# When the maxima of batch 0's v, their factor and two conversion factors come later in the program

## The chip, the cores and the metric

The kernel runs on one core of a Trainium2 chip. The metric is the time of one execution on the device in microseconds (us). The engines go by short names: PE is TensorE (matmuls and transposes), DVE is VectorE, ACT is ScalarE, POOL is GpSimd, and SP is the queue that issues the DMA transfers.

## The reference

Causal attention over 4 batches of 12 heads (448 tokens, 64 values a head), then a feed-forward layer with a leaky ReLU, then a soft mixture of eight experts:

```python
scores = scale * np.matmul(q, k.transpose(0, 1, 3, 2))
scores = np.where(mask, -1000000000.0, scores)
attn = softmax(scores)                      # over the keys
x = heads side by side of np.matmul(attn, v)   # 1792 x 768
h = x @ w_in                                # 768 x 2048
g = np.maximum(0.01 * h, h)
x = g @ w_out                               # 2048 x 768
...
logits = x @ phi                            # 768 x 32, then 8 experts of 4 slots each
return c @ slot_out                         # 1792 x 768
```

## The kernel before

The work is cut into four stages. In stage 0 (the first 100 us) the attention of batch 0 runs alone; in stages 1 to 3 the attention of batch b runs between the feed-forward matmuls of batch b-1; then come the last batch and the experts. The change touches stage 0 alone.

**Attention.** Two heads make a pair; batch 0 has pairs 0 to 5. Step n of the attention has three slots, which end at a `yield`. In step n the engines make the weights of pair n, the row maxima of pair n+1 and the product of pair n-1 with v. For pair n, in order: `qkps` (PE transposes q and k; ACT copies them, DVE subtracts for a low part, both into `qkt`); `S_3`, `S_0`, `S_1` (PE scores for the maxima, tiles 3, then 0 and 2, then 1) and `junk` on DVE, which leaves the maxima in `mxe`; `mps` (PE transposes `mxe`); `mr` (ACT, four instructions); `T_0`, `T_1`, `T_2` (PE, the scores less their maxima); `P` (ACT, the exponential; one for each T); a mask on `P` by POOL (L449) after T_1 and after T_2; `tsum` on POOL (L454, then L458 twice); `O` (PE, the product with v; its second half reads the P of T_2); `dn` (PE, the sums), `r` (DVE, reciprocal), `rb` (PE) and `rs` (ACT); at the end DVE multiplies `O` by `rs` and by batch 0's factor `s_v` (L520), and ACT and POOL split the result into the two halves of `x16`. S and T share two PSUM buffers, O has one.

**Factor of v.** `reduce_v(n)` takes the largest |v| of pair n (DVE, L370). `v_scale(b)` takes the largest over six pairs (L375), multiplies it with the identity on PE to bring it to all partitions (`v_ps`, L140), and makes the factor with five small DVE instructions. Batch 0's six maxima and its factor stand ahead of step 0 in the program.

**Conversions.** Six blocks of w_in, i0 to i5, are turned from doubles into two halves of 16 bits each in stage 0. `prep_in` is a generator; prep_step lets it go on once before (BEFORE) and once behind (AFTER) each slot. One conversion is: ACT takes the magnitude (`cv`) and the sign (`cs`) of the raw block; DVE takes its maximum (`w_am`, L228), shifts (L229) and joins the low word (L230); two AFTERs later PE multiplies the maximum with the identity (`w_ps`) and DVE makes the factor `w_s`; then ACT scales `cs` by it, POOL multiplies `cv` by `cs` (L249), ACT or POOL casts the high half of `w`, and POOL subtracts for the low half (L258). There are two buffers for `cs`, four for `cv`, three for the raw blocks.

**What sets the order.** On PE every matmul that goes through `mm` keeps the order of the program (`in_order`). On DVE, ACT, POOL and SP the order in stage 0 is that of a scheduler which plays the program through once with its own costs, except where `tc.issue_after` ties an instruction behind another. Attention slots have a higher priority (AHEAD) than conversions. At run time each engine takes its instructions strictly in the order so fixed.

Of the kernel before, what the change touches and what calls it, by code (L numbers as in the profile page):

```python
# [29 lines left out]
def as_float(bits):  # L30
    return struct.unpack("<f", struct.pack("<I", bits))[0]
# [3 lines left out]
def tile_attn_moe_softmoe(ctx: ExitStack, tc: tile.TileContext, q, k, v, w_in, w_out, phi, w1, w2, out, dbg=None):  # L35
    nc = tc.nc
# [10 lines left out]
    NP = H // 2  # L47
# [10 lines left out]
    ident = const.tile([128, 128], F32, name="ident")  # L58
# [29 lines left out]
    def ps_tr(name, shape=(128, 512)):  # L88
        return psum.tile(list(shape), F32, tag="tr", bufs=TR[0], name=name)
# [4 lines left out]
    def last_on(engine):  # L94
        return next(i for i in reversed(nc.cur_bb.bb.instructions[-400:]) if i.engine == engine)
# [35 lines left out]
    mm = partial(in_order, nc.tensor.matmul)  # L131
# [3 lines left out]
    def pow2_scale(absmax, name, shift=23, bias=0, out=None):  # L135


        ps = ps_tr(f"{name}_ps", (128, 128))
        op = nc.tensor.matmul if name == "v0" else mm
        op(ps, absmax.to_broadcast([128, 128]), ident, start=True, stop=True)  # L140
        m1 = const.tile([128, 1], F32, tag="p2_m1", bufs=2, name=f"{name}_m1")
        nc.vector.tensor_reduce(m1, ps, AX.X, ALU.max)
        nc.vector.tensor_scalar(m1, m1, as_float((27 + bias) << shift), None, ALU.max)
        e = const.tile([128, 1], I32, tag="p2_e", bufs=2, name=f"{name}_e")
        nc.vector.tensor_scalar(e, m1.bitcast(I32), shift, None, ALU.logical_shift_right)
        si = const.tile([128, 2], I32, tag="p2_s" + name[0], bufs=4, name=f"{name}_s")
        nc.vector.tensor_scalar(si[:, 0:1], e, -(2**23), (268 + bias) * 2**23, ALU.mult, ALU.add)
        if out is None:
            out = si[:, 1:2].bitcast(F32)
        nc.vector.tensor_scalar(out.bitcast(I32), e, 2**23, -(14 + bias) * 2**23, ALU.mult, ALU.add)  # L150
        return si.bitcast(F32)[:, 0:1], out
# [85 lines left out]
    def prep_in(u):  # L237

        f = u[1]
        am = const.tile([128, 1], F32, tag="w_am", bufs=2, name=f"w_am{f}")  # L240
        t, sg = to_f32(u, am)
        yield AFTER
        yield AFTER
        s_w, _ = pow2_scale(am, f"w{f}", 20, out=inv_w[:, f : f + 1])
        yield BEFORE
        if u[3]:
            yield BEFORE
        scalar.activation(sg, sg, AF.Copy, scale=s_w)
        nc.gpsimd.tensor_tensor(t, t, sg, ALU.mult)  # L249
        if u[3]:  # L250
            yield BEFORE
        w = t.rearrange("p (c f) -> p c f", c=NP)
        hi, lo = (w16[f // 4][:, x, :, 128 * (f % 4) : 128 * (f % 4 + 1)] for x in range(2))
        if f < EARLY[0] and f % 4 < HIP:
            nc.gpsimd.tensor_copy(hi, w)
        else:
            scalar.copy(hi, w)
        nc.gpsimd.tensor_tensor(lo, w, hi, ALU.subtract)  # L258
        ready.add(u[:2])
# [44 lines left out]
    BEFORE, AFTER = "before", "after"  # L304
# [58 lines left out]
    def reduce_v(n):  # L363

        b, hp = divmod(n, NP)
        if hp == 0:
            v_am[b] = am = const.tile([128, NP + 1], F32, tag="v_am", bufs=2, name=f"v_am{b}")
            nc.vector.memset(am, 0.0)
        with tc.issue_after(last_on(mybir.EngineType.DVE)) if b else ExitStack():
            nc.vector.tensor_reduce(v_am[b][:CP, hp : hp + 1], v_t[n], AX.XY, ALU.max, apply_absolute_value=True)  # L370

    def v_scale(b):

        am = v_am[b]
        nc.vector.tensor_reduce(am[:, NP:], am[:, :NP], AX.X, ALU.max)  # L375
        s_v[b], inv_v[b] = pow2_scale(am[:, NP:], f"v{b}")
# [177 lines left out]
    def attention_slots():  # L554


        for n in range(2):
            qk_stacks(n)
            load_qk(n + 2)
            if n == 0:  # L560
                for tiles in TILES:
                    maxima(0, tiles)
        for x in range(NP):
            reduce_v(x)
        v_scale(0)
        for n in range(NP + 1):
            here, more = n < NPAIR, n + 1 < NPAIR
            if n > 0:
                attend(n - 1)
            if here:  # L570
                lowering(n)
            if more:
                maxima(n + 1, TILES[0])
            if here:
                weights(n, 0)
            yield
            if n > 0:
                inverses(n - 1)
            if more:
                maxima(n + 1, TILES[1])  # L580
            if here:
                weights(n, 1)
            yield
            if n > 0:
                columns(n - 1)
            if here:
                weights(n, 2)
            if more:
                maxima(n + 1, TILES[2])
            if n + 2 < NPAIR:  # L590
                qk_stacks(n + 2)
                if n + 4 < NPAIR:
                    load_qk(n + 4)
            if n + NP < NPAIR:
                load_v(n + NP)
            if NP <= n + NP - 1 < NPAIR:
                reduce_v(n + NP - 1)
            yield

        for n in range(NP + 1, NPAIR + 1):  # L600
            here, more = n < NPAIR, n + 1 < NPAIR
            if more:
                maxima(n + 1, TILES[2])
            attend(n - 1)
            inverses(n - 1)
            if here:
                lowering(n)
            yield
            if here:
                weights(n, 0)  # L610
            if more:
                maxima(n + 1, TILES[0])
            if n % NP == 1 and n + NP - 2 < NPAIR:
                v_scale(n // NP)
            yield
            if here:
                weights(n, 1)
                weights(n, 2)
            if more:
                maxima(n + 1, TILES[1])  # L620
            if n + 2 < NPAIR:
                qk_stacks(n + 2)
                if n + 4 < NPAIR:
                    load_qk(n + 4)
            if n + NP < NPAIR:
                load_v(n + NP)
            columns(n - 1)
            if n + NP - 1 < NPAIR:
                reduce_v(n + NP - 1)
            yield  # L630

    TILES = ((3,), (0, 2), (1,))
    slots_of_attention = attention_slots()


# [213 lines left out]
    if True:  # L849
# [123 lines left out]
        for c in range(4):  # L973
            wo = loaded.pop(("wo", c))
            for h in range(2):
                for t in range(4):
                    nc.tensor.matmul(
                        psi[h][32 * t : 32 * t + 32], gdt[:, c, t], wo[:, t, 384 * h : 384 * (h + 1)],
                        start=c == 0, stop=c == 3, skip_group_check=True,
# [18 lines left out]
        for e in range(E):  # L998
            ph = ps2(f"ph{e}", (128, 256), tag="h", bufs=4)
            for hf in range(2):  # L1000
                wt = loaded.pop(("w1", (e, hf)))
                for t in range(3):
                    rows = wt[:, t].rearrange("k (p t) -> k p t", t=8)
                    for g in range(4):
# [3 lines left out]
                            start=hf == 0 and t == 0, stop=hf == 1 and t == 2, skip_group_check=True,  # L1008
# [87 lines left out]
        for x, (t0, nt, c0, cols) in enumerate(pieces):  # L1096
# [11 lines left out]
            for h in heads:  # L1108
                for t in range(nt):
# [3 lines left out]
                        start=t0 + t < 4, stop=t0 + t >= 8 * E - 4, skip_group_check=True,  # L1113
# [65 lines left out]
```

## Time and profile before

| | us |
|---|---|
| three runs | 646.23, 647.52, 650.63; median 647.52 |
| the profiled execution | 647.08 |
| its span in the trace | 645.40 |
| PE busy in the span | 579.7 (90%) |
| PE busy in 0 to 20, 20 to 40, 40 to 60 us | 7.72, 14.13, 17.78 of 20 each |
| POOL busy in 40 to 60 and 60 to 80 us | 15.99, 16.09 of 20 each |

The span runs from the first to the last instruction in the trace; the execution's own time holds 1.68 us more around it. PE's busy share is high over the whole, so what a change in the first 100 us is worth has to be read there: which engine each engine waits for in that stretch, and at what time the same instruction of each step starts.

### The profile page before, as it was taken

How to read it: one execution, taken by the hardware profiler on the slowest of the kernel's cores; microseconds unless marked ns; L12 is line 12 of the kernel's file. 1: busy time of each engine (PE TensorE's matmuls, PEld its weight loads, DVE VectorE, ACT ScalarE, POOL GpSimd, SP SyncE). 2: the span in 40 equal slices, each digit the busy share in tenths (PEclk: the TensorE clock that was granted, in tenths of full speed). 3: DMA queues.
4: the chain of work that ended last, by engine and by line, in shares of the span. 5: the costliest groups of instructions: out<-in, count | busy, mean ns of one | idle time of the engine just before them, and what ended most of it. 6: DMA issues, size and time to landing. Idle time of an engine off the chain costs nothing.

```text
span 645.4 us, 12376 instructions
## 1 busy us (share of the span) xinstructions
PE 579.7 (90%) x4874; PEld 333.8 (52%) x4874; DVE 367.5 (57%) x884; ACT 290.2 (45%) x570; POOL 235.3 (36%) x247
## 2 busy tenths in 40 slices
PE   3688888997999999999999999999999998999564
PEld 2455555654545566556656655554344445454233
DVE  5868757989965666656358667424657423001023
ACT  2566655678765657656446546432022112011012
POOL 5177973488585465435434334430000000000000
PEclk9989999998999999999999999999999998899998
DMA  9942237764552366653434312216969539999998
GB/s 183 283 112 66 59 77 200 217 164 132 144 162 72 107 180 217 190 158 100 113 106 104 110 56 68 75 39 231 356 244 412 194 132 422 407 423 423 408 328 316
DMA packets 108849, 125.67 MB, mean 195 GB/s; under 512 B 69368, under 2 KB 99064, under 8 KB 105208
## 3 DMA queue, kind: packets, MB, share of 16 engines
q1 hardware_dynamic: 108792, 124.90, 59.9%
q8 instruction: 38, 0.62, 0.4%
q14 instruction: 19, 0.16, 0.1%
HBM read 105.74 MB, written 19.14 MB: 193 GB/s over the span
## 4 chain that ended last, share of the span: by engine, by line
PE 64%; DMA 10%; POOL 8%; DVE 6%; ACT 6%; issue 3%; SPq 2%; ACTq 0%; POOLq 0%; DVEq 0%
PE H L102 30%; DMA w<-in_moe_w_dram 7%; PE O L102 5%; PE T L102 5%; PE g_acc L102 3%; PE dn L102 3%; PE L L102 2%; PE S L102 2%; PE qkps L102 2%; PE ph L1005 2%; DMA raw_i_None<-in_moe_w_in_dram 2%; PE wt_ps L102 2%; POOL w L258 2%; ACT P L113 2%; DVE cv_i_None L230 1%
## 5 line engine op out<-in xcount | busy, mean ns | idle before, releaser
L102 PE MATMUL H<-x,w 128*128 128x448 f16 x1152 | 229.8, 353 | 0.7 <-ACT g L113 0.7
L102 PEld LDWEIGHTS <-w 128*128 128x128 f16 x1152 | 111.0, 99 | 110.9 <-issue 17.8
L409 DVE CUSTOM_DVE_ANT_0 junk<-S,mask 112x224 bf16<-112x224 f32 (+3 forms) x192 | 85.2, 444 | 58.9 <-PE S L102 55.9
L487 DVE RECIPROCAL rs<-rs 128x224 f32<-128x224 f32 x36 | 53.4, 1524 | 40.6 <-ACT rs L113 40.6
L113 ACT ACTIVATE P<-T 112x672 f32<-112x672 f32 (+1 forms) x72 | 57.0, 793 | 22.0 <-PE T L102 20.9
L449 POOL TENSOR_SCALAR_AFFINE_SELECT P<-P 112x448 f32<-112x448 f32 x48 | 30.8, 643 | 91.2 <-ACT P L113 71.0
L102 PE MATMUL T<-qkt 64*112 64x336 f32 (+3 forms) x576 | 60.1, 321 | 4.4 <-ACT P L113 3.6
L113 ACT ACTIVATE g<-H,iv 128x448 f32<-128x448 f32 x48 | 30.5, 635 | 67.6 <-PE H L102 48.3
L102 PE MATMUL O<-P,v 112*64 112x448 f32 (+3 forms) x384 | 52.0, 410 | 4.5 <-POOL P L449 4.4
L102 PEld LDWEIGHTS T<-qkt 64*112 64x112 f32 x576 | 42.8, 180 | 14.6 <-issue 6.0
L458 POOL TENSOR_TENSOR tsum<-tsum,P 112x448 f32<-112x448 f32 (+1 forms) x48 | 47.4, 987 | 1.9
L102 PEld LDWEIGHTS O<-P,v 112*64 112x64 f32 x384 | 25.2, 138 | 29.2 <-issue 11.9
L454 POOL TENSOR_TENSOR tsum<-P 112x672 f32<-112x672 f32 x24 | 39.1, 1630 | 1.8
L102 PE MATMUL S<-qkt 64*112 64x224 f32 (+3 forms) x192 | 31.6, 369 | 7.6 <-DVE mxe L409 2.9
L997 POOL MEMSET hz<- 128x256 f32 x2 | 0.6, 312 | 97.7 <-PE g_acc L102 97.7
L113 ACT ACTIVATE g_spare<-H,iv 128x448 f32<-128x448 f32 x16 | 10.2, 635 | 56.7 <-PE H L102 56.7
L387 DVE TENSOR_TENSOR qkt<-qkps,qkt 128x448 fp32r<-128x448 f32 x48 | 29.1, 621 | 9.7 <-ACT qkt L113 9.7
L102 PE MATMUL T<-mr,onesr 64*112 64x448 f32 (+1 forms) x192 | 30.7, 316 | 4.3 <-ACT mr L113 4.3
L249 POOL TENSOR_TENSOR cv_i_None<-cv_i_None,cs_i_None 128x768 f32<-128x768 f32 x16 | 28.6, 1786 | 11.1 <-ACT cs_i_None L113 11.1
L113 ACT ACTIVATE mr<-mps,own 128x112 fp32r<-128x112 f32 x96 | 26.2, 361 | 14.0 <-PE mps L102 14.0
L113 ACT COPY rs<-dn 128x448 f32<-128x448 f32 x18 | 9.6, 533 | 50.5 <-PE dn L102 47.5
L267 POOL TENSOR_TENSOR cv_o_None<-cv_o_None,cs_o_None 128x768 f32<-128x768 f32 x10 | 16.5, 1647 | 42.4 <-DVE cv_o_None L230 18.4
(176 smaller groups left out, 906.8 us busy)
## 6 DMA issues: line engine op xcount, KB each, us to landing
w<-in_moe_w_dram SPq DMA_DIRECT2D x31, 1536.0 KB
raw_i_None<-in_moe_w_in_dram SPq DMA_DIRECT2D x16, 768.0 KB
raw_o_None<-in_moe_w_out_dram SPq DMA_DIRECT2D x10, 768.0 KB
g_far<-g SPq DMA_DIRECT2D x32, 224.0 KB
gb<-g_far SPq DMA_DIRECT2D x8, 896.0 KB
wo<-wsc SPq DMA_DIRECT2D x4, 1536.0 KB
qk<-in_q_dram SPq DMA_DIRECT2D x48, 112.0 KB
qk<-in_k_dram SPq DMA_DIRECT2D x48, 112.0 KB
```

The source lines that it names most:

```text
L102: op(*args, **kwargs)
L113: op(*args, **kwargs)
L249: nc.gpsimd.tensor_tensor(t, t, sg, ALU.mult)
L258: nc.gpsimd.tensor_tensor(lo, w, hi, ALU.subtract)
L267: nc.gpsimd.tensor_tensor(wo, wo, sg, ALU.mult)
L387: nc.vector.tensor_tensor(st[:, j, 1], p, st[:, j, 0].bitcast(F32), ALU.subtract)
L409: nc.vector.tensor_tensor_reduce(out=junk[:, :w], in0=ps[:, a, at : at + w], in1=mask[:, S - w :], scale=-1.0, scalar=3e38, op0=ALU.add, o ...
L449: nc.gpsimd.affine_select(out=d, in_=d, compare_op=ALU.is_ge, fill=0.0, base=0, pattern=[[0, 4], [1, CP]], channel_multiplier=-1,)
L454: nc.gpsimd.tensor_tensor(tsum[:CP], p[0][:CP, :, 0, CP:], p[0][:CP, :, 1, : S - CP], ALU.add)
L458: nc.gpsimd.tensor_tensor(y, y, p[1][:CP, :, j, : S - CP * (j + 2)], ALU.add)
L487: nc.vector.reciprocal(rs[:, c : c + S // 2], rs[:, c : c + S // 2])
L1005: nc.tensor.matmul(ph[32 * g : 32 * g + 32].rearrange("s (p u) -> s p u", u=2), sit[:, 3 * hf + t], rows[:, :, 2 * g : 2 * g + 2], start=h ...
```

## The change

The six reductions of batch 0's v leave the place ahead of step 0. Two of them come into the second slot of step 0, four into the third, and the factor into the third slot of step 1. Each reduction is tied behind the DVE instruction that the program issued last before it. The product `v_ps` goes through `mm`, so it now has its fixed place among PE's instructions. For i0 and i1 the product `w_ps` comes two slots later than before.

```diff
         ps = ps_tr(f"{name}_ps", (128, 128))
-        op = nc.tensor.matmul if name == "v0" else mm
-        op(ps, absmax.to_broadcast([128, 128]), ident, start=True, stop=True)
+        mm(ps, absmax.to_broadcast([128, 128]), ident, start=True, stop=True)
...
         yield AFTER
         yield AFTER
+        if f < 2:
+            yield AFTER
+            yield AFTER
         s_w, _ = pow2_scale(am, f"w{f}", 20, out=inv_w[:, f : f + 1])
...
+        behind = last_on(mybir.EngineType.DVE)
         if hp == 0:
...
-        with tc.issue_after(last_on(mybir.EngineType.DVE)) if b else ExitStack():
+        with tc.issue_after(behind):
             nc.vector.tensor_reduce(v_am[b][:CP, hp : hp + 1], v_t[n], AX.XY, ALU.max, apply_absolute_value=True)
...
-        for x in range(NP):
-            reduce_v(x)
-        v_scale(0)
         for n in range(NP + 1):
...
+            if n == 0:
+                reduce_v(0)
+                reduce_v(1)
             yield
+            if n == 1:
+                v_scale(0)
             if n > 0:
                 columns(n - 1)
...
+            if n == 0:
+                for x in range(2, NP):
+                    reduce_v(x)
```

The scheduler's order changes with it on every engine in stage 0. PE, ahead of step 0, before (`v0_ps` is the product of v's maximum, `mps0` the transpose of pair 0's maxima; the digit after a name is the pair or conversion):

```order
L102 MATMUL qkps1_1_241<-ident_64,qk1_162 128x112 x4
L140 MATMUL v0_ps_262<-ident_64,v_am0_253 128x128
L102 MATMUL mps0_272<-ident_64,mxe0_142 128x112
L102 MATMUL S1_3_279<-qkt1_233 112x448 x2
L102 MATMUL T0_0_286<-qkt0_186 112x448 x6
```

PE, in step 1, of the changed kernel:

```order
L102 MATMUL T1_1_447<-qkt1_233 112x336 x6
L102 MATMUL T1_1_447<-mr1_391,onesr_120 112x336 x2
L139 MATMUL v0_ps_464<-ident_64,v_am0_312 128x128
L102 MATMUL rb0_474<-r0_432,first_131 64x112 x8
L102 MATMUL T1_2_489<-qkt1_233 112x224 x6
```

The product with v's maximum has left the place ahead of `mps0` and stands behind T_1 of pair 1, in front of `rb0`.

ACT, from the first `mr` on, before:

```order
L113 ACTIVATE mr0_274<-mps0_272,own_123 128x112 x4
L113 ACTIVATE cv_i0_None_297<-raw_i0_None_179 128x768
L113 ACTIVATE cs_i0_None_298<-raw_i0_None_179 128x768
L113 ACTIVATE cv_i1_None_396<-raw_i1_None_181 128x768
L113 ACTIVATE cs_i1_None_397<-raw_i1_None_181 128x768
L113 ACTIVATE P0_448_144<-T0_0_286 112x2x448
L113 ACTIVATE cv_i2_None_557<-raw_i2_None_183 128x768
L113 ACTIVATE P0_448_144<-T0_1_319 112x2x336
```

and in the changed kernel:

```order
L113 ACTIVATE mr0_255<-mps0_253,own_123 128x112 x4
L113 ACTIVATE P0_448_144<-T0_0_267 112x2x448
L113 ACTIVATE P0_448_144<-T0_1_300 112x2x336
L113 ACTIVATE cv_i0_None_278<-raw_i0_None_179 128x768
L113 ACTIVATE cs_i0_None_279<-raw_i0_None_179 128x768
L113 ACTIVATE P0_224_145<-T0_2_316 112x2x336
L113 ACTIVATE cv_i1_None_371<-raw_i1_None_181 128x768
L113 ACTIVATE cs_i1_None_372<-raw_i1_None_181 128x768
```

The first two exponentials of pair 0 no longer stand behind two conversions.

ACT, in step 2, of the changed kernel (in the kernel before, only `cv_i5` stands between these two exponentials):

```order
L113 ACTIVATE P0_448_144<-T2_0_585 112x2x448
L113 ACTIVATE cs_i1_None_372<-cs_i1_None_372,w1_s_559 128x768
L113 ACTIVATE cs_i2_None_544<-cs_i2_None_544,w2_s_606 128x768
L113 ACTIVATE cv_i4_None_871<-raw_i4_None_378 128x768
L113 CAST w16_0_97<-cv_i1_None_371 128x6x128
L113 ACTIVATE cs_i3_None_716<-raw_i3_None_285 128x768
L113 CAST w16_0_97<-cv_i2_None_543 128x6x128
L113 ACTIVATE cs_i4_None_872<-raw_i4_None_378 128x768
L113 ACTIVATE P0_448_144<-T2_1_633 112x2x336
```

POOL, at the same place, in the changed kernel:

```order
L461 TENSOR_TENSOR tsum_148<-tsum_148,P1_224_147 112x2x112
L251 TENSOR_TENSOR cv_i1_None_371<-cv_i1_None_371,cs_i1_None_372 128x768
L251 TENSOR_TENSOR cv_i2_None_543<-cv_i2_None_543,cs_i2_None_544 128x768
L260 TENSOR_TENSOR w16_0_97<-cv_i1_None_371,w16_0_97 128x6x128
L260 TENSOR_TENSOR w16_0_97<-cv_i2_None_543,w16_0_97 128x6x128
L452 AFFINE_SELECT P0_448_144<-P0_448_144 112x4x112
L457 TENSOR_TENSOR tsum_148<-P0_448_144 112x672
L525 TENSOR_TENSOR x16_0_485<-rs1_658,x16_0_485 128x448
L452 AFFINE_SELECT P0_224_145<-P0_224_145 112x4x112
```

The four POOL instructions of i1 and i2 stand together between step 1 and step 2; before, i1's stand in step 1 and i2's in step 2, and i0's in step 0 instead of step 1. From step 4 on the orders of PE, ACT and POOL are those of before (but for one transpose of PE near the end of the program), and DVE's differ in a few single instructions.

## Rows read from the trace of the kernel before

**Rows 1.** The chain that ended last, 20 to 66 us, summed by line.

```profile
by line: DMA raw_i_None<-in_moe_w_in_dram 29.1%; issue 18.1%; POOL tsum L458 11.3%; POOL cv_i_None L249 10.6%; POOL tsum L454 10.6%; POOL w L258 10.6%; POOL P L449 8.3%; POOL x L522 4.4%; ACT cv_i_None L113 3.9%; ACT P L113 2.0%; ACT cs_i_N
```

**Rows 2.** PE's timeline: start, length (us), instruction, count, idle before and its releaser.

```profile
17.63 0.77 PE L140 MATMUL v_ps<-ident,v_am 128*128 128x128 f32 x2 [6.38 <-DVE v_am L375]
18.19 0.39 PE L102 MATMUL mps<-ident,mxe 112*128 112x112 f32 x1
...
25.00 1.18 PE L102 MATMUL T<-qkt 64*112 64x336 f32 x6 [3.56 <-ACT P L113]
...
40.52 1.76 PE L102 MATMUL rb<-r,first 128*64 128x112 f32 x16
...
44.06 0.36 PE L102 MATMUL S<-qkt 64*112 64x224 f32 x2 [0.66 <-DVE mxe L409]
...
47.30 0.32 PE L102 MATMUL mps<-ident,mxe 112*128 112x112 f32 x1
...
52.41 0.99 PE L102 MATMUL rb<-r,first 128*64 128x112 f32 x16 [0.59 <-DVE r L497]
...
58.22 0.32 PE L102 MATMUL mps<-ident,mxe 112*128 112x112 f32 x1
...
61.84 0.41 PE L102 MATMUL dn<-tsum,sixteen 128*64 128x112 f32 x4 [0.52 <-POOL tsum L458]
```

**Rows 3.** ACT's timeline, conversions and the first exponential.

```profile
20.21 0.91 ACT L113 ACTIVATE cv_i_None<-raw_i_None 128x768 f32<-128x768 f32 x1 [0.43 <-DMA raw_i_None<-in_moe_w_in_dram]
...
24.05 0.89 ACT L113 ACTIVATE P<-T 112x896 f32<-112x896 f32 x1
...
42.76 0.94 ACT L113 ACTIVATE cs_i_None<-cs_i_None,w_s 128x768 bf16<-128x768 bf16 x1
```

**Rows 4.** DVE's timeline, the last maximum of pair 0.

```profile
13.39 0.08 DVE L409 DVE_READ_ACCUMULATOR2_ANT mxe<- 112x1 f32 x1
```

**Rows 5.** DVE by line, 0 to 110 us: count, then busy us, mean ns, idle before.

```profile
L409 DVE CUSTOM_DVE_ANT_0 junk<-S,mask 112x224 bf16<-112x224 f32 (+3 forms) x66 | 29.2, 442 | 10.3 <-PE S L102 9.2
L387 DVE TENSOR_TENSOR qkt<-qkps,qkt 128x448 fp32r<-128x448 f32 x18 | 10.6, 621 | 9.7 <-ACT qkt L113 9.7
L370 DVE TENSOR_REDUCE v_am<-v 112x1 f32<-112x512 f32 x13 | 8.9, 681 | 2.5 <-DMA v<-in_v_dram 2.5
L228 DVE TENSOR_REDUCE w_am<-cv_i_None 128x1 f32<-128x768 f32 x7 | 6.6, 938 | 0.6 <-ACT cv_i_None L113 0.6
L230 DVE SCALAR_TENSOR_TENSOR cv_i_None<-raw_i_None,cv_i_None 128x768 int32<-128x768 int32 x6 | 5.6, 935 | 0.0
...
L497 DVE RECIPROCAL r<-dn 128x112 f32<-128x112 f32 x6 | 5.1, 852 | 0.7 <-PE dn L102 0.7
L229 DVE TENSOR_SCALAR cv_i_None<-cv_i_None 128x768 int32<-128x768 int32 x6 | 4.3, 718 | 0.1
L520 DVE SCALAR_TENSOR_TENSOR rs<-O,v_s,rs 128x448 f32<-128x448 f32 x6 | 4.1, 682 | 1.0 <-ACT rs L113 1.0
```

**Rows 6.** Timeline of POOL and DVE, side by side.

```profile
27.96 1.61 POOL L454 TENSOR_TENSOR tsum<-P 112x672 f32<-112x672 f32 x1
...
28.41 1.58 DVE L229 TENSOR_SCALAR cv_i_None<-cv_i_None 128x768 int32<-128x768 int32 x1
```

**Rows 7.** POOL's timeline.

```profile
33.57 1.65 POOL L249 TENSOR_TENSOR cv_i_None<-cv_i_None,cs_i_None 128x768 f32<-128x768 f32 x1
...
45.92 1.05 POOL L522 TENSOR_TENSOR x<-rs,x 128x448 f16<-128x448 f32 x1
...
48.03 1.66 POOL L258 TENSOR_TENSOR w<-cv_i_None,w 128x768 f16<-128x768 f32 x1
...
56.85 0.59 POOL L449 TENSOR_SCALAR_AFFINE_SELECT P<-P 112x448 f32<-112x448 f32 x1
```

**Rows 8.** Stretches of 2 us: length, then busy (count) of PE, PEld, DVE, ACT, POOL; granted clock.

```profile
36.00:38.00 2.00, 0.82 (x6) 0.48 (x6) 0.00 (x0) 1.45 (x6) 1.92 (x2) 1.00 0.28 52
...
40.00:42.00 2.00, 2.00 (x22) 1.55 (x18) 1.97 (x11) 0.73 (x1) 0.56 (x1) 0.50 0.07 25
```

## The prediction

> **What bounds the kernel now.** I read the chain of work first, over 20 to 66 us. The reader is to see that no PE line is among its large shares: the five POOL lines of attention and conversions hold 11.3 + 10.6 + 10.6 + 10.6 + 8.3 + 4.4, some 56% of the stretch, and the landing of the first raw blocks 29% [rows 1]. So stage 0 is a pipeline that POOL paces once the blocks have landed. Then PE's timeline, for the waits at its start: 6.38 us until the six maxima of v are in, and 3.56 us in front of T_1 of pair 0, for the first exponential [rows 2]. That exponential starts at 24.05, because two conversions stand before it on ACT, and the first of them waits for its block until 20.21 [rows 3]. The marks by which I measure progress are the same instructions of each step: S_1 at 44.06, mps of pair 2 at 47.30, mps of pair 3 at 58.22 [rows 2]. From step 4 on PE, ACT and POOL have their old order, so a shift that stands there is carried to the end one for one; the later stages have no timetable of their own.
>
> **Removed: the wait for v, and the conversions before the first exponential.** The last maximum of pair 0 is read out at 13.39 to 13.47, and two of v's reductions (0.68 each) lie ahead of it on DVE [rows 4, 5]. Without them mps of pair 0 can run at about 13.0 (an estimate: part of their time is a wait for ACT's copies in any case) instead of 18.19 [rows 2], which is 5.2 us. Its exponentials follow at once, so the 3.56 us go too: some 8.5 us in all, if nothing else were late. Nothing of it is worth more than what comes next on the other engines, so I follow DVE and then POOL.
>
> **DVE takes the work back.** The magnitude of i0 still cannot be there before 20.21 + 0.91 = 21.1 [rows 3], and behind it DVE now has an unbroken run. Until the factor w_s of i0: three conversions' DVE part, each 0.94 + 0.55 + 0.94 (the shift's mean of 0.72 holds one long case; the other five have (4.3 - 1.58)/5 = 0.54) make 7.3; four reductions of v 2.7; six `junk`, 0.44 each and 0.08 for the read-out, 3.1; two `qkt` 1.2; the reciprocal 0.85; the small ones about 1.0, an estimate from their number, seven of 0.15 [rows 4 to 6]. That is 16.2, so w_s of i0 is there at 37.3. Two more `junk` and some small ones end at 38.5, and S_1 of pair 2 follows on PE: 38.5 against 44.06, still 5.5 us ahead. The factor of v costs nothing here beyond its DVE time, which is in the sum: PE waits for `rb` and S_1 at that place in any case, and `v_ps` is ready before T_1 is done. Behind `v_ps` on PE stand `rb`, T_2 and S_1; all wait for DVE's run, not for it. Then `rs` 0.68, two `junk` 1.0, two `qkt` 1.2, a reduction of v 0.68, i3's part 2.4, two `junk` 1.3 and small ones 0.8 bring w_s of i1 to 46.5.
>
> **POOL, and the two conversions that meet in step 2.** i0's factor moves later, so POOL can begin its product only at 37.3 + 0.94 for the scaling of the signs = 38.2, against 33.57 before [rows 3, 7]. POOL loses there 4.6 of the microseconds that PE has won. Before pair 2's first mask it must do both products and both low halves of i1 and i2, and this begins with w_s of i1: 46.5 + 0.94 + 4 x 1.65 + mask 0.59 + tsum 1.61 + x 1.05 + mask 0.59 = 57.9 [rows 3, 6, 7]. ACT takes the same path: between two exponentials of step 2 it has seven instructions instead of one, and one of them casts what POOL has just made, so the exponential of T_1 ends near 53.5. Before, that last mask ended at 56.85 + 0.59 = 57.44 and mps of pair 3 came 0.78 later [rows 2, 7]; now 57.9 + 0.8 = 58.7 against 58.22. So all 5.5 us are given back within step 2, and 0.5 more.
>
> **What DVE and POOL do to each other.** One shift on DVE took 1.58 instead of 0.54 us: it began while POOL's tsum ran and ended 0.42 after it, at 29.99 against 29.57 [rows 6]. In the new order, POOL's tsum of pair 1 runs at about 35 to 36.7, beside i2's joining on DVE, and i0's low half at about 43.3 to 45, beside i3's shift. No row shows a joining (L230) begin beside a running POOL instruction. By the one row each place costs 0 to 1.0 us, so 0 to 2.0 together; I take 1.0, since the shift is the form that was seen to wait and the joining is not. The Trainium skill, page "SBUF — State Buffer", section "Who interferes with whom", says that DVE and GpSimd share one pair of ports as an exclusive lock, and that a DVE instruction with two inputs in SBUF meets it too. By that rule both places would wait and the sum would be about 1 us higher than mine.
>
> **The sum.** mps of pair 3: 0.5 later from the chain above, and 1.0 for the wait between DVE and POOL: +1.5. In the trace of before the sums `dn` then waited 0.52 us for POOL's last tsum [rows 2], which now comes behind no low half; that wait goes: some -0.6. Net +0.9 on the profiled execution's 647.08, so **648.0 us**. The runs shown have a median of 647.52 and reach from 646.23 to 650.63, so the profiled execution is one of the middle. About 1% (6.5 us) is what a measurement of this kernel can tell from no change, and I forecast no change. The parts not priced: the transpose that changes places near the end, and single DVE reductions of later batches, stand in work with slack on both sides; they get 0, with a few tenths either way if that cover is gone. On the SP queue the fourth raw block now goes behind the loads of pair 4's q and k, some 2 us later than before by the places of its neighbours (an estimate). Its magnitude stands on ACT between the first and the second exponential of pair 1, and T_1 of that pair, which waits for DVE's run until 32 to 33.5, hides it; if that cover is gone it costs those 2 us at S_1 of pair 2, where 5.5 are in hand.
>
> **Rivals.** (1) The lead is kept. If the two conversions of step 2 fill time in which PE waits for nothing, the lead at mps of pair 2 stands to the end. S_1 at 38.5, then 0.4 for itself, 1.7 for qkps (slow like the `rb` of that time), 0.5 for w_ps of i1 and 2.1 for O give 43.3 against 47.30 [rows 2], 4.0 us: 647.1 - 4.0 = 643.1. For it: POOL was idle at several places in each step, as the 18% "issue" in the chain shows [rows 1]. Against it: the exponential of T_1 stands behind all of them on ACT, in strict order. (2) Slower, by PE's clock. In step 2 PE waits some 2.9 us in front of `rb` and 2.3 in front of T_2. In the trace of before, a stretch with PE busy for only 0.82 of 2 us (36 to 38) was followed by one at a granted clock of 0.50 (40 to 42), the level of 1.2 GHz [rows 8]; `rb` took 1.76 there and 0.99 in the next step [rows 2]. T_2, S_1, qkps and O of one step, 4.1 us at the full clock, would take some 6.4 (an estimate: up to 1.8 times as long, as `rb`, and less where weight loads set the pace). This decides once T_2 starts later than about 53: then PE and no longer POOL is last, and mps of pair 3 comes at 55.4 + 6.4 = 61.8, net +3.0: 650.1. The Trainium skill, "TensorE: Matmul & The Clock Gate", section "What's actually happening", says the low level is the default and activity lifts it; by that rule this rival holds if the two waits count as idle. (3) All is kept: 647.1 - 8.5 = 638.6, if DVE's run is far shorter than my sum. Against it: the sum is made of measured lengths. (4) The change does not do what it says, and the wait for v only moves to `v_ps` in step 1: PE would then stand there until L375, which I place at 29; `v_ps` comes at 33.5. The price is nil, and the time as in the forecast.
>
> **How the numbers follow.** Forecast, within -1.5 and +1.5 of 648.0: 0.46, with 0.03 of it for (4). Rival 1: 0.22. Rival 2: 0.25. Rival 3: 0.04. The rest, 0.03, is for what the later stages might make of a shift. The range takes in rivals 1 and 2 at their centres with half a microsecond for the runs' spread: 642.8 to 650.6. Only rival 3 and a part of the rest are over 1% faster: 0.05; over 1% slower is a part of rival 2 and of the rest: 0.03; 0.92 lie within 1%.
>
> **What would show it.** In the profile of the changed kernel: mps of pair 0 at 13 (first step right); S_1 of pair 2 near 38.5 with DVE without a gap from 21 to 38 (second); POOL's first product near 38 and four conversion instructions in a row between 46 and 55 (third); the exponential of T_1 of pair 2 ending near 53.5 and mps of pair 3 between 58 and 62. If mps of pair 3 is at 54 to 55, rival 1 is right; if PE's granted clock falls to 0.50 around 52 to 58, rival 2. The forecast is wrong if DVE's run is broken by waits that I did not see, or if w_s of i1 comes well before 46.

## The result, and the profile after

The changed kernel takes 656.25 us (median of 12 runs, 653.33 to 659.74) against 649.51 of the kernel before beside it (12 runs, 646.23 to 654.77): ratio 1.0109, 95% interval 1.0087 to 1.0130. It is slower by about 1.1%, and outside my range. The profiled execution has a span of 654.0 us, before 645.40.

I write mps(n) for mps of pair n, and so on for the other names, and follow the shift of mps(n) against before: -5.60 us at mps(0), -8.63 at mps(1), -7.72 at mps(2), then **+3.58 at mps(3)**, +3.67 at mps(4), +4.03 at mps(6), **+6.74 at mps(7)**, and 6.9 to 7.0 from mps(8) to the last pair at 417 us. So two stretches lose: 11.3 us between mps(2) and mps(3), 2.7 between mps(6) and mps(7). The rest of the span's 8.6 (1.7) arises near 600 us in this one execution; the medians are 6.7 apart, so I leave it out.

PE's timeline of the changed kernel answers to [rows 2]; columns as there.

```profile
12.59 0.42 PE L102 MATMUL mps<-ident,mxe 112*128 112x112 f32 x1 [1.23 <-DVE mxe L412]
...
35.52 0.36 PE L102 MATMUL S<-qkt 64*112 64x224 f32 x2
...
39.58 0.31 PE L102 MATMUL mps<-ident,mxe 112*128 112x112 f32 x1
...
44.27 0.41 PE L102 MATMUL dn<-tsum,sixteen 128*64 128x112 f32 x4 [1.59 <-POOL tsum L461]
...
50.21 1.76 PE L102 MATMUL rb<-r,first 128*64 128x112 f32 x16 [2.98 <-DVE r L500]
54.23 0.90 PE L102 MATMUL T<-qkt 64*112 64x224 f32 x6 [2.26 <-DVE mxe L412]
...
57.87 4.00 PE L102 MATMUL O<-P,v 112*64 112x448 f32 x16
61.80 0.45 PE L102 MATMUL mps<-ident,mxe 112*128 112x112 f32 x1
...
107.20 0.53 PE L102 MATMUL S<-qkt 64*112 64x224 f32 x2 [2.24 <-DVE qkt L390]
107.66 4.00 PE L102 MATMUL O<-P,v 112*64 112x448 f32 x16
```

The gain is there up to 39.58. In step 2 three waits follow that before did not have in this size, and then everything on PE is slow: O takes 4.00 us. What the waits are for stands on DVE and POOL, side by side.

```profile
39.80 3.90 DVE L228 TENSOR_SCALAR cv_i_None<-cv_i_None 128x768 int32<-128x768 int32 x1
...
45.64 0.14 DVE L146 TENSOR_SCALAR w_s<-w_e 128x1 int32<-128x1 int32 x1
...
48.44 0.95 DVE L227 TENSOR_REDUCE w_am<-cv_i_None 128x1 f32<-128x768 f32 x1 [1.78 <-ACT cv_i_None L113]
49.31 0.85 DVE L500 RECIPROCAL r<-dn 128x112 f32<-128x112 f32 x1
...
50.67 2.21 DVE L229 SCALAR_TENSOR_TENSOR cv_i_None<-raw_i_None,cv_i_None 128x768 int32<-128x768 int32 x1
```

```profile
39.54 1.04 POOL L525 TENSOR_TENSOR x<-rs,x 128x448 f16<-128x448 f32 x1
40.53 1.14 POOL L461 TENSOR_TENSOR tsum<-tsum,P 112x448 f32<-112x448 f32 x1
41.63 1.65 POOL L260 TENSOR_TENSOR w<-cv_i_None,w 128x768 f16<-128x768 f32 x1
43.24 0.98 POOL L461 TENSOR_TENSOR tsum<-tsum,P 112x224 f32<-112x224 f32 x1
46.82 3.24 POOL L251 TENSOR_TENSOR cv_i_None<-cv_i_None,cs_i_None 128x768 f32<-128x768 f32 x2 [2.61 <-ACT cs_i_None L113]
50.02 4.36 POOL L260 TENSOR_TENSOR w<-cv_i_None,w 128x768 f16<-128x768 f32 x2
...
57.56 0.58 POOL L452 TENSOR_SCALAR_AFFINE_SELECT P<-P 112x448 f32<-112x448 f32 x1
```

i3's shift, 0.54 us long elsewhere, begins at 39.80 beside POOL's x and ends at 43.70. It was held: it stood on DVE far longer than its own work takes, while POOL worked. Three POOL instructions follow each other without a gap until 43.28; the shift got its turn behind the third, and the fourth then takes 0.98 instead of 0.67. Behind it on DVE stands i1's factor (45.64), behind that ACT's scalings of cs, behind these ACT's magnitude of i4, for which DVE waits at 48.44 with `r` behind it, for which PE waits at 50.21. i4's joining is held too, 2.21 instead of 0.94, but only by one instruction: the first low half ends at 52.07, the joining at 52.88, and the second low half, which begins at 52.02, takes 2.36 instead of 1.65. On ACT seven conversion instructions stand ahead of the exponential of T_1(2).

```profile
45.81 1.82 ACT L113 ACTIVATE cs_i_None<-cs_i_None,w_s 128x768 bf16<-128x768 bf16 x2 [3.32 <-DVE w_s L146]
...
51.63 0.72 ACT L113 ACTIVATE P<-T 112x672 f32<-112x672 f32 x1
```

Stretches of 2 us, columns as in [rows 8]: PE's granted clock falls to 0.50, its lower level, when these waits begin, and a second time ahead of O(6).

```profile
42.00:44.00 2.00, 0.68 (x12) 0.46 (x12) 2.00 (x2) 0.49 (x1) 2.00 (x2) 1.00 1.13 320
44.00:46.00 2.00, 1.08 (x10) 0.70 (x12) 2.00 (x9) 0.19 (x1) 0.21 (x1) 0.82 0.21 32
46.00:48.00 2.00, 1.23 (x8) 0.78 (x8) 0.56 (x5) 2.00 (x3) 1.18 (x1) 0.50 0.00 0
...
60.00:62.00 2.00, 2.00 (x13) 1.12 (x9) 0.00 (x0) 0.00 (x0) 0.10 (x1) 0.50 0.61 138
...
104.00:106.00 2.00, 0.96 (x10) 0.75 (x8) 1.02 (x6) 1.66 (x4) 2.00 (x2) 1.00 1.09 365
106.00:108.00 2.00, 0.80 (x4) 0.55 (x6) 1.97 (x4) 0.39 (x1) 1.84 (x4) 0.68 1.19 290
108.00:110.00 2.00, 2.00 (x8) 0.71 (x6) 0.60 (x5) 0.00 (x0) 0.64 (x1) 0.50 0.91 138
```

Three causes offered themselves for the 11.3 us: the held shift, the two conversions that stand together on ACT and POOL, and the clock. The experiments take them one by one.

### The profile page after: what moved, and what is told of

Its sections match the earlier page's. It is cut to its first block, busy times and chain, and to the rows that moved or that the text cites. A ratio compares the mean times of both kernels' runs of the same rounds, so it can differ in the third digit from the quotient of the medians.

```text
span 654.0 us, 12378 instructions
## 1 busy us (share of the span) xinstructions
PE 588.2 (90%) x4874; PEld 336.2 (51%) x4874; DVE 369.6 (57%) x884; ACT 290.2 (44%) x570; POOL 237.5 (36%) x247
## 4 chain that ended last, share of the span: by engine, by line
PE 65%; DVE 13%; DMA 8%; ACT 5%; POOL 4%; issue 3%; SPq 1%; POOLq 0%; ACTq 0%; DVEq 0%
PE H L102 29%; DMA w<-in_moe_w_dram 8%; PE O L102 7%; PE T L102 5%; DVE cv_i_None L229 3%; PE g_acc L102 3%; PE dn L102 2%; PE S L102 2%; PE L L102 2%; DVE junk L412 2%; PE qkps L102 2%; PE wt_ps L102 2%; PE ph L1013 2%; ACT P L113 2%; DVE rs L490 1%
## 5 line engine op out<-in xcount | busy, mean ns | idle before, releaser
L102 PE MATMUL O<-P,v 112*64 112x448 f32 (+3 forms) x384 | 57.2, 443 | 4.8 <-POOL P L452 4.8
L102 PEld LDWEIGHTS T<-qkt 64*112 64x112 f32 x576 | 43.1, 182 | 16.2 <-DVE mxe L412 6.0
L102 PEld LDWEIGHTS O<-P,v 112*64 112x64 f32 x384 | 27.3, 148 | 32.6 <-issue 15.2
```

The lines of the kernel that those rows point to most:

```text
L102: op(*args, **kwargs)
```

## The experiments

Shifts of mps(n) in us against the profile of before; "2 to 3" is the time from mps(2) to mps(3); the ratio is to the kernel before on the same chip, with its 95% interval.

| kernel | 2 to 3 | mps(2) | mps(3) | mps(5) | mps(8) | ratio |
|---|---|---|---|---|---|---|
| before | 10.92 | 0 | 0 | 0 | 0 | 1 |
| changed | 22.22 | -7.72 | 3.58 | 3.55 | 6.95 | 1.0109 (1.0087-1.0130) |
| a1 v moved alone | 11.14 | -3.07 | -2.85 | -2.79 | 0.25 | 0.9994 (0.9965-1.0022) |
| a2 delay alone | 22.07 | -2.07 | 9.08 | 9.05 | 12.27 | 1.0188 (1.0151-1.0225) |
| a3 delay of one slot | 14.66 | -0.18 | 3.56 | 3.39 | 7.02 | 1.0142 (1.0087-1.0197) |
| f1 DVE order | 19.96 | -5.11 | 3.93 | 4.85 | 6.99 | 1.0134 (1.0098-1.0169) |
| f2 ACT order | 19.48 | -6.88 | 1.68 | 3.23 | 6.77 | 1.0051 (1.0022-1.0079) |
| f3 both orders | 17.32 | -5.25 | 1.15 | 2.50 | 5.93 | 1.0069 (1.0042-1.0097) |
| f5 and POOL's order | 15.97 | -6.45 | -1.40 | 3.23 | 5.28 | 1.0094 (1.0059-1.0130) |
| g1 idle products, too many | 24.51 | -7.97 | 5.62 | 6.54 | 8.12 | 1.0116 (1.0058-1.0174) |
| g2 idle products, sized | 19.35 | -8.12 | 0.31 | 0.13 | 1.67 | 1.0051 (1.0015-1.0088) |
| h1 a1 + 27 idle products | 11.13 | -4.00 | -3.79 | -3.79 | -2.92 | 0.9958 (0.9926-0.9989) |
| h2 a1 + 20 idle products | 11.13 | -3.19 | -2.98 | -2.97 | -1.88 | 0.9970 (0.9947-0.9992) |
| c0 before + 20 | 10.99 | -1.41 | -1.34 | -1.33 | -0.05 | 0.9996 (0.9974-1.0019) |
| f4 f3 + 20 | 19.63 | -7.19 | 1.52 | 2.87 | 3.96 | 1.0053 (1.0026-1.0080) |
| f6 f5 + 20 | 15.35 | -6.39 | -1.96 | 3.95 | 5.04 | 1.0049 (1.0015-1.0082) |

Each row of marks comes from one trace. How far such traces scatter can be seen where two kernels have the same instructions in the same order up to a mark: c0's mps(2) is 1.41 us ahead of that of before, and f4's is 1.94 ahead of f3's, ahead of any idle product; f3 and f4 differ by 2.3 in "2 to 3" and by 0.4 at mps(3). A difference of less than some 2 us between two rows shows nothing by itself.

**Which half costs.** a1 leaves out the delay:

```diff
-        if f < 2:
-            yield AFTER
-            yield AFTER
```

> Only the move of batch 0's v is kept; the products of i0's and i1's maxima with the identity stand where they stood. Theory of the held shift (the two conversions' late factors put GpSimd instructions back to back, i3's shift on the DVE waits for all of them, w1's factor and all behind it stand still): no such clump here, so i3's shift takes under 2 us, most of the lead of 5 to 8 us at mps(1) and mps(2) is carried, and the span is 638 to 643 us, ratio 0.985 to 0.995. Rival that the moved maxima of v are what costs (a DVE run that comes back later): slower than before, 650 to 656 us, with or without the delay.

a2 is the kernel before with those three lines.

> Only the two-slot delay of i0's and i1's products is made; v stays ahead of the first step. The GpSimd order in steps 1 and 2 is the changed kernel's. Held shift: i3's shift meets the same run of GpSimd instructions and takes 2.5 to 4 us, mps(3) is 3 to 11 us later than before and the span is 649 to 656 us, ratio 1.005 to 1.017. Rival that v's move costs: within 0.5% of before, 643 to 648.

The delay costs: a2 loses 11.15 us between mps(2) and mps(3), as the changed kernel does, and is 1.9% slower, more than expected; a1 loses 0.2 there, and none of its six shifts in stage 0 takes over 1.06 us. At mps(8) the changed kernel is 5.3 us ahead of a2: beside the delay, moving v pays. But my ratio for a1 was missed: its lead of 2.8 us is gone by mps(8), so there is a second loss that has nothing to do with the delay. In a2 it was not the shift that was held (0.83 us) but i3's joining, 2.89.

a3 has one `yield AFTER` in place of the two.

> The changed kernel with a delay of one slot instead of two, so that i1's second half (scaling, product, high half, low half) no longer falls into the slot of i2's. Theory of the clump (after a two-slot delay i1's and i2's second halves meet in one slot of step 2; ScalarE then has seven conversion instructions in a row ahead of the exponentials of T_1(2), and the DVE has r(1) and the maxima of S_3(0) behind i4's maximum, which waits for ScalarE): from mps(2) to mps(3) it takes 10.5 to 12 us as before (10.92) and not 22.2, mps(3) is at 50 to 54, and unless the clock falls elsewhere the span is 637 to 643. Rival that any delay of these products costs, by the held shift or by buffers that come free later: 16 to 22 us between the two, span 650 to 655.

Missed. i1's second half no longer meets i2's, yet 14.66 us pass, and in step 1, where POOL now has i0's product, i2's shift is held for 2.88 us; PE then waits 3.31 ahead of S_1(2). 14.66 lies between the two expectations, and the span, 656.6, is past the rival's 650 to 655: the shorter delay too put POOL instructions in a row beside a shift.

**Is it the order in the queues?** f1 queues i3's shift behind what is needed:

```diff
-        nc.vector.tensor_scalar(ti, ti, 3, None, ALU.logical_shift_left)
+        with tc.issue_after(marks["w1"]) if (kind, f) == ("i", 3) else ExitStack():
+            with tc.issue_after(marks["S3"]) if (kind, f) == ("i", 3) else ExitStack():
+                nc.vector.tensor_scalar(ti, ti, 3, None, ALU.logical_shift_left)
```

> The changed kernel, with i3's shift and joining queued on the DVE behind w1's factor and behind the maxima of S_3(3); the order on the other engines is unchanged, and so is every instruction. Held shift: the shift still waits for GpSimd, but nothing that is needed waits behind it: w_s1 at about 41 instead of 45.6, ScalarE's first scaling of cs at about 41.3 instead of 45.8, mps(3) at 54 to 58.5 instead of 61.8, span 646 to 651 against 654 of the changed kernel (ratio to before 1.00 to 1.008). Rival that two conversions side by side on GpSimd and ScalarE cost the time by themselves: w_s1 is early, but mps(3) stays at 61 to 62 and the span at 653 to 655. Rival that the fall of TensorE's clock alone costs it: as long as TensorE waits as often, 0.50 again and 653 to 655.

PE's timeline of f1, and DVE's:

```profile
50.51 1.26 PE L102 MATMUL rb<-r,first 128*64 128x112 f32 x16 [3.97 <-DVE r L507]
55.32 0.91 PE L102 MATMUL T<-qkt 64*112 64x224 f32 x6 [3.55 <-DVE mxe L417]
...
62.15 0.32 PE L102 MATMUL mps<-ident,mxe 112*128 112x112 f32 x1
```

```profile
44.28 1.10 DVE L233 TENSOR_SCALAR cv_i_None<-cv_i_None 128x768 int32<-128x768 int32 x1
...
48.74 0.95 DVE L230 TENSOR_REDUCE w_am<-cv_i_None 128x1 f32<-128x768 f32 x1 [1.78 <-ACT cv_i_None L113]
49.61 0.85 DVE L507 RECIPROCAL r<-dn 128x112 f32<-128x112 f32 x1
```

The shift is down to 1.10 us and w_s of i1 is at 44.16, 2.0 us behind mps(2) instead of 6.1, but mps(3) is not earlier: PE's two waits are longer, since `r` still stands behind i4's maximum and that behind ACT's conversions. The held shift alone is not the cause; my first theory falls. The test is not quite clean: i2's factor, at 46.74, now stands behind the shift and i3's joining, and ACT's second scaling waits 1.05 us for it.

f2 puts later conversion work behind what PE waits for: on ACT behind the exponential of T_1(2) (P21), on DVE behind the maxima of S_0(3) (S32; the texts on record call it S_3(0)). i1's casts also come one yield later:

```diff
+        with behind("P21") if late else ExitStack():
+            scalar.activation(t, hw.bitcast(F32), AF.Abs, scale=2.0**-112)
...
+            with behind("S32") if late else ExitStack():
+                nc.vector.tensor_reduce(absmax, t, AX.X, ALU.max)
...
+        if f == 1:
+            yield BEFORE
...
+            with behind("P21") if f in (1, 2) else ExitStack():
+                scalar.copy(hi, w)
```

> The changed kernel with the same instructions in another order in step 2: on ScalarE the exponentials of T_1(2) stand right behind the two scalings, ahead of the high halves of i1 and i2, cs of i3 and i4 and cv of i4 (these five were ahead of it); on the DVE i4's maximum, shift and joining stand behind r(1) and the maxima of S_3(0); TensorE's order is the same, and on GpSimd x stands behind the two low halves. Clump theory: the wait ahead of rb falls from 2.98 to under 1, the one ahead of T_2(2) from 2.26 to under 1, the clock holds 1.00 from 50 us, mps(3) at 53 to 56 instead of 61.8 and the span at 645 to 650 (two parts of the eleven lost remain: i3's held shift and the second halves on GpSimd). Rival that GpSimd's eight conversion instructions are the bound: mps(3) at 60 to 62, span 653 to 656.

The waits ahead of rb(1) and T_2(2) fell to 0.25 and 0 as expected. But mps(3) is at 59.90, next to the rival's 60 to 62 and not at 53 to 56: the shift took 4.26 us, the clock fell with PE's wait of 1.59 for `tsum`, and O(2) then waited 2.97 for `rs`, behind ACT's next conversions.

```profile
55.97 4.00 PE L102 MATMUL O<-P,v 112*64 112x448 f32 x16 [2.97 <-DVE rs L544]
```

f3 has both orders, with i4's work behind the copy of rb(1) on ACT and behind `rs` on DVE.

> The changed kernel with both reorderings: on the DVE i3's shift behind w1's factor and the maxima of S_3(3), and i4's maximum, shift and joining behind r(1), the maxima of S_3(0) and the scaling of O(1); on ScalarE the exponentials of T_1(2) right behind the two scalings, and cs of i3, cv and cs of i4 behind the copy of rb(1). Each alone left the time between mps(2) and mps(3) long (19.96 us with the first, 19.48 with the second, 22.22 with none, 10.92 before). If both queues are what holds it, each sufficient by itself: with both gone 11 to 14 us, mps(3) at 51 to 55, a lead of 3 to 7 us at mps(5), of which the end of the stage may take 2 to 3 as with v alone; span 640 to 646, ratio 0.985 to 1.0. If the rest is bound by GpSimd (its run of products and low halves) or by buffers that come free later: 16 to 20 us, mps(3) at 56 to 60, span 650 to 654.

f3's timelines of PE and of POOL:

```profile
50.78 0.99 PE L102 MATMUL qkps<-ident,qk 112*128 112x112 f32 x8
52.22 1.54 PE L102 MATMUL O<-P,v 112*64 112x448 f32 x8 [0.45 <-POOL tsum L480]
58.05 1.39 PE L102 MATMUL O<-P,v 112*64 112x224 f32 x8 [4.30 <-POOL P L475]
59.37 0.45 PE L102 MATMUL mps<-ident,mxe 112*128 112x112 f32 x1
```

```profile
45.95 4.04 POOL L267 TENSOR_TENSOR cv_i_None<-cv_i_None,cs_i_None 128x768 f32<-128x768 f32 x2
49.95 0.57 POOL L475 TENSOR_SCALAR_AFFINE_SELECT P<-P 112x448 f32<-112x448 f32 x1
50.60 1.62 POOL L480 TENSOR_TENSOR tsum<-P 112x672 f32<-112x672 f32 x1
52.18 3.26 POOL L279 TENSOR_TENSOR w<-cv_i_None,w 128x768 f16<-128x768 f32 x2
55.39 1.36 POOL L552 TENSOR_TENSOR x<-rs,x 128x448 f16<-128x448 f32 x1
56.70 1.30 POOL L475 TENSOR_SCALAR_AFFINE_SELECT P<-P 112x448 f32<-112x448 f32 x1
```

The rival holds. From mps(2) on PE works at the full clock and waits under 1 us at a time up to 53.8, then 4.30 for a mask that POOL reaches only after a run from 46. f5 moves the two low halves behind that mask and T_2(2)'s partial sums, and i4's and i5's work on ACT and DVE further back:

```diff
-        nc.gpsimd.tensor_tensor(lo, w, hi, ALU.subtract)
...
+        if f in (1, 2):
+            yield BEFORE
+        with behind("t2") if f in (1, 2) else ExitStack():
+            nc.gpsimd.tensor_tensor(lo, w, hi, ALU.subtract)
```

> The kernel with both reorderings, and now on GpSimd the low halves of i1 and i2 behind the mask and the partial sums of T_2(2); on ScalarE cs of i3, cv and cs of i4 and cv of i5 behind the exponentials of T_2(2), on the DVE i4's maximum behind the maxima of S_1(3). TensorE's order is unchanged. If the place of the second halves ahead of the mask is what is left: the wait of 4.30 us for the mask falls under 1, mps(2) to mps(3) takes 11 to 13 us, mps(3) is at 52 to 55; as GpSimd then owes 3.3 us of low halves to step 3, mps(4) may give 0 to 3 us of that back. Span 641 to 648, ratio 0.987 to 0.998. If two conversions in one step are too much for GpSimd in any order: what is gained at mps(3) is lost by mps(5), where the lag is 1 to 4 us as now, and the span is 649 to 654.

mps(3) is 1.40 us ahead of before (56.82), and mps(4) is 3.51 behind it. In step 3 POOL now has the low halves beside i4's shift, and DVE's row there reads:

```profile
56.43 3.94 DVE L244 TENSOR_SCALAR cv_i_None<-cv_i_None 128x768 int32<-128x768 int32 x1
```

Its casts of `qkt` and the maxima wait behind it. The second reading holds: what is gained at mps(3) is lost again by mps(4). f6 adds idle products to f5.

> The same with 8 idle products of TensorE ahead of O(4) and 12 ahead of O(5). If the place was the cause: 1 to 2 us better than without them, span 639 to 646, ratio 0.985 to 0.996, the best of the versions with the delay. If GpSimd's amount of work is: within 1 us of the run without them or 1 to 2 better, 648 to 653.

It gains 0.2 us at mps(8) in the profile and 1.3 in the medians (653.76 after 655.06); its interval and f5's overlap.

**The clock.** g1 and g2 keep PE busy in the waits of step 2 with products that are overwritten or unused:

```diff
+            if n == 1:
+                keep(rb, 30)
...
+            if n == 1:
+                keep(ps_tr("keep", (128, S)), 20)
```

> The changed kernel with 30 idle products into the tile of rb ahead of rb(1), and 20 into a tile of their own behind it (their results are not used), so that TensorE works through its waits for r and for mxe. Clock theory (what was lost from 46 to 62 us is the fall to 0.50): the clock is back at 1.00 by 52 us, rb, the transposes and O take 0.99, 0.90 and 2.1 instead of 1.76, 1.76 and 4.00, mps(3) at 58.5 to 59.5, span 650 to 652. Held shift alone: the waits are as long and mps(3) gains under 1 us, span 653 to 655. Together they would put about 3 of the 11.3 us lost between mps(2) and mps(3) on the clock and the rest on the waits.

Too many: each product is two passes in the trace, and the 30 took 8.2 us, over the wait's end. But from the first product of T_2(2) to mps(3) it took 4.06 us (59.78 to 63.84) against 7.57 in the changed kernel. g2 has 11 and 12.

> The idle products of the run before, sized to the waits: 11 ahead of rb(1) and 12 behind it (30 and 20 overran the waits by some 5 us). Clock theory: mps(3) follows the first product of T_2(2) by 4.1 us, as at full clock in the run before, and not by 7.6; with that product at 54 to 55 mps(3) is at 58 to 59, the lag at steps 4 and 5 is 0 to 1 us instead of 3.6, span 650 to 652. If the clock is not the cause of those 3.5 us: mps(3) at 61 to 62 and the span at 654.

PE's timeline of g2:

```profile
53.84 0.57 PE L102 MATMUL T<-qkt 64*112 64x224 f32 x6 [0.74 <-DVE mxe L412]
...
58.53 0.31 PE L102 MATMUL mps<-ident,mxe 112*128 112x112 f32 x1
```

As the clock theory expects up to mps(5): T_2(2) starts 0.39 us earlier than in the changed kernel, mps(3) 3.27. So about 3 of the 11.3 us are the clock's and 8 the waits'. The span is 648.5, below the 650 to 652 expected, but this was the fastest of ten executions: their median is 653.97, where before has 651.61 on the same chip. The ratio is 1.0051 after 1.0109.

**The second loss.** In a1 most of the lead goes at O(6), as in the changed kernel: of 2.79 us at mps(5), 0.88 go by mps(6), with the clock at 0.50 behind O(4), and 2.15 by mps(7). PE's timeline of before, and of a1:

```profile
80.61 0.79 PE L102 MATMUL O<-P,v 112*64 112x224 f32 x8 [1.79 <-POOL P L449]
...
103.26 0.36 PE L102 MATMUL S<-qkt 64*112 64x224 f32 x2 [1.18 <-DVE qkt L387]
103.54 2.11 PE L102 MATMUL O<-P,v 112*64 112x448 f32 x16
```

```profile
101.80 0.36 PE L102 MATMUL S<-qkt 64*112 64x224 f32 x2 [1.62 <-DVE qkt L387]
102.09 3.80 PE L102 MATMUL O<-P,v 112*64 112x448 f32 x16
```

h1 is a1 with 8 idle products ahead of O(4), 12 ahead of O(5) and 7 ahead of S_1(8):

```diff
+        if n == 8 and tiles == (1,):
+            keep(ps[:64, 0, :CP], 7)
...
+        keep(o[:64, :CP], {4: 8, 5: 12}.get(n, 0))
```

> The kernel with v alone moved, and idle products of TensorE (results overwritten) in its three longest waits at the end of stage 0: 8 ahead of O(4), 12 ahead of O(5), 7 ahead of S_1(8). With v alone moved the lead of 2.9 us at mps(5) was gone at mps(7), and there O(6) took 3.80 us at a clock of 0.56 where before has 2.11 at 1.00. Clock theory: with TensorE kept busy O(6) takes 2.1, the lead at mps(7) is 2 to 3.5 us, and the span 642.5 to 645, ratio 0.992 to 0.997. Rival that the stage's end is set by something else that comes at a fixed time (a transfer, the last conversions): mps(7) stays at before's within 0.5 us, and the ratio within 0.998 to 1.002.

PE's timeline of h1:

```profile
98.85 1.55 PE L102 MATMUL S<-ident,sixteen 128*64 128x112 f32 x14 [2.24 <-DVE qkt L387]
100.33 0.36 PE L102 MATMUL S<-qkt 64*112 64x224 f32 x2
100.62 2.11 PE L102 MATMUL O<-P,v 112*64 112x448 f32 x16
```

O(6) takes 2.11 us, 2.9 us of lead reach mps(8), and the kernel is 0.4% faster than before. Of this lead 0.9 us more than a1's was there at mps(2), ahead of the products. h1 and h2 are the only ones that beat both kernels. h2 leaves out the 7, c0 is the control.

> v alone moved, with the 8 and the 12 idle products ahead of O(4) and O(5), without the 7 ahead of S_1(8), which themselves waited 2.24 us for the DVE there and then took 1.5 in the way of S_1(8). If the first two keep the clock by themselves, O(6) takes 2.1, the lead of 3.8 us at mps(5) stands at mps(7) within 0.4, and the ratio is 0.993 to 0.996; if the wait of 1.6 ahead of S_1(8) still drops the clock, O(6) takes 3.8 and the ratio is 0.997 to 1.001.

> Control: the kernel before, with the same 8 and 12 idle products and v where it stood. If the 0.4% that the kernel with v moved and idle products won comes from moving v, this one is at 0.998 to 1.002 (in before's profile the clock fell there only at 94 to 97 us, for some 0.7 us of work); if it comes from the idle products alone, 0.993 to 0.997.

In h2 O(6) takes 3.53 again, after a wait of 2.23, and 1.1 us of lead goes (ratio 0.9970); c0 is the same as before. h1 loses 0.9: its seven products keep the clock, but take 1.5 us themselves, so they win little. h2 and c0 ran on one chip, with medians of 648.29 and 649.74, though their intervals overlap: the gain needs the move of v, and the 20 idle products alone give nothing. f4 is f3 with the 20.

> The kernel with both reorderings and, besides, 8 idle products of TensorE ahead of O(4) and 12 ahead of O(5). Clock theory of the stage's end: O(6) at 2.1 us instead of 3.8 to 4.0, the lead at mps(7) as large as at mps(5) within 0.7 us, 2 to 3 us better there than the kernel with the reorderings alone: span 638 to 644. If idle products only cost: 0 to 2 us worse.

Its mps(8) is 2.0 us earlier than f3's; between mps(5) and mps(8) it loses 1.1 us, f3 3.4. The other pairs agree: 3.0 in a1 and 1.1 in h2, 2.1 in f5 and 1.1 in f6. But O(6) takes 3.80, not the 2.1 expected, the ratios' intervals overlap, and 638 to 644 us was far off, for f3's lead was never there.

## Why the prediction was wrong

**The first step was right**: mps(0) at 12.59 (predicted 13.0), and the wait for the first exponential down from 3.56 to 0.30.

**The second had the mechanism and too long a run**: S_1(2) at 35.52 instead of 38.5, DVE without a gap up to that point. i0's magnitude was there earlier, nothing was held, and the run up to i0's factor took 13.7 us (20.5 to 34.2), not 16.2. The lead at mps(2) was 7.7 us, not rival 1's 4.0.

**The fourth step, "What DVE and POOL do to each other", failed in its size.** I gave each place 0 to 1.0 us and took 1.0 for both. The one row that I had showed a shift beside a single POOL instruction [rows 6]; beside several in a row the price can be that of more than one. i3's shift lost 3.36 us and i4's joining 1.27, 4.6 together. The place of i3's shift was right; the joining that I placed beside `tsum` (i2's, at 33.4) ended before `tsum` began and was not held, i4's was. The Trainium skill, "SBUF — State Buffer", "Who interferes with whom", says that a DVE form with two inputs in SBUF meets a GpSimd instruction that reads SBUF, and that `tensor_scalar` can, in a two-port mode; the trace agrees that both waited, with 2.21 us for the joining and 3.90 for the shift. That alone still does not make the forecast wrong: i1's factor came at 45.64, against 46.5, since the shorter run and the longer hold cancel; and f1 shows that without the hold the time is no better.

**The third step, two conversions that meet in step 2, is where the forecast failed: it took POOL for the engine that ends last, and PE's clock at nothing.** The four conversion instructions in a row are there, 46.8 to 54.4, and the exponential of T_1(2) ends at 52.35 (predicted 53.5). From there I followed POOL's masks alone. POOL's path came out as summed: the last mask ended at 58.14, against 57.9, and in g2, where the clock is kept, mps(3) follows that mask at 58.53, against the 58.7 of the sum. But in the changed kernel PE was last, some 3 us behind that path. Left out were DVE's waits: i4's maximum waits for ACT and has `r` behind it, and its joining is held ahead of most maxima of S_0(3). So T_2(2) starts at 54.23, later than the 53 that I had named as the point from which rival 2 decides, and at the low clock it takes 7.57 us from there to mps(3). The 0.6 us that I took off for `dn` did not come either: in step 3 PE's wait ahead of S_1(4) grew from 0.61 to 1.48 in its place.

**So rival 2 came, at 0.25, and not the forecast.** Its mps(3) of 61.8 is what was measured (61.80), granted clock 0.50 from 46 to 62. That the two agree so closely is luck: rival 2 had T_2(2) 1.2 us too late, at 55.4, and the slow stretch behind it 1.2 too short, 6.4. g2 prices it at about 3 us. Rival 1's lead was not kept to mps(4) in any kernel with the delay.

**"A shift that stands there is carried to the end one for one" failed as well**, and this is why 650.1 was still too low: +3.67 at mps(4) became +6.95 at mps(8). The step had a wait of 1.18 ahead of S_1(8) before; in the changed kernel it is 2.24, the clock falls, and from O(6) to mps(7) it takes 5.42 us instead of 2.80. a1 and h1 show it without the delay: O(6) at 3.80 against 2.11. In a1 the longer wait and the slower O(6) take 2.1 of the 2.8 us that moving v had won.

What is shown: the delay is what costs (a1 and a2), the clock has about 3 of the 11.3 us and most of the 2.7, and in each order tried the work that waits for i0's and i1's factors came up again as a wait: on DVE, on ACT, on POOL's mask, in step 3. From mps(2) to mps(3) POOL has five conversion instructions (i0's low half, two products, two low halves) where before has two by the same marks. That POOL's amount of work sets a floor in any possible order is argued from these and not shown; other orders were not tried.

## What to carry to other kernels

Work taken out of a queue's idle time early on comes back later as a run, and what meets the run (a DVE form that waits for GpSimd, as the shift did here, an in-order queue behind it) can pay for several of its instructions, not for one: sum the run, and ask which engine is then last. A lead is only worth what passes the next long wait of TensorE: a few idle products there can cost less than the slow products behind it, if they end before the wait does. Test the halves of a two-part change apart; here one was worth 0.3 to 0.4% with idle products beside it and nothing without them, and the other cost 1.9% alone.

## What the runs showed of the hardware

A DVE shift of 0.5 us that began beside a POOL instruction got its turn only behind the third in a row: 3.90 us here and 3.94 in f5; in a3 behind the second, 2.88, in f2 behind the fourth, 4.26. It is not always so: i4's joining here (2.21) and i4's shift in f3 (53.98 to 55.86) got theirs behind the one instruction that they had met, in the middle of a run, and the next POOL instruction was the longer one. What decides is not shown.

And one wait of PE can decide what the next products cost. Ahead of S_1(8) it waited 1.18 us in before, and O(6) took 2.11 at a granted clock of 1.00; after 1.62 to 2.24 us in c0, a1, h2 and the changed kernel the clock fell, and O(6) took 2.65 to 4.00. In h1 it held through 2.24 us, with seven idle products right behind the wait; in h2, the same kernel without these seven, it fell. The length of one wait does not settle it: 1.79 us ahead of O(4)'s second half was followed by 1.00 in before (80.61) and by 0.50 in a1 (77.75).
